# Longformer attention and an MoE layer on one core: where bias adds, gathers, stores and roundings stand in the order

## The chip, the cores and the metric

The kernel runs on one core of one Trainium2 chip. A core has TensorE (PE, matmuls), VectorE (DVE), ScalarE (ACT), GpSimd (POOL) and SyncE (SP, which here only issues transfers); each works through a queue of its own in program order, and semaphores make one wait for another. Matmuls write PSUM, the other engines move results from there to SBUF. The metric is the device time of one execution in microseconds (us). Before the change three timed runs took 341.11 us in the median (341.09 to 342.33).

## The reference

Attention over q, k, v of shape (8, 8, 576, 64) with a mask: a query sees keys within 32 positions, and 8 global positions see and are seen by all. The result, as 4608 tokens of 512, goes through two dense layers with a squared ReLU between them.

```python
mask = np.abs(pos[:, None] - pos[None, :]) <= window          # window = 32
mask = mask | is_global[:, None] | is_global[None, :]
scores = np.where(mask, scale * (q @ k.T), -1e9)
attn = softmax(scores);  x = attn @ v                          # per head
h = x @ w_in                                                   # 512 -> 2048
g = s * np.maximum(h, 0.0) ** 2 + b
out = g @ w_out                                                # 2048 -> 512
```

## The kernel before

The work on attention runs over 32 pairs of heads (four pairs to one of the 8 batches), each pair in 8 steps that are called s = 0 to 7 here. The dense layers are cut into 9 blocks of 512 tokens; a block is 16 pieces that make a slice of h (`psh`, L728), which ACT passes through ReLU into `r` (L750) and DVE squares into `g` (L753), and 16 pieces that multiply by w_out (`pso`, L762). These pieces are called quanta; `Q` puts one or more of them between the steps of attention, so that PE has work while the other engines do exp, masks and evictions. All engines are scheduled by hand: what stands earlier in the program stands earlier in the engine's queue.

A pair's way: its q and k rows are loaded by SP (`load_nat`, `load_q`, L213 and L234), rounded to bf16 by ACT (`round_k` L224 into `natb`, `round_q` L249 and L254 into `sixq`), and transposed, the keys of pairs from 8 on by a transposing transfer of SP (`turn_k`, L260, into `kt`), the queries by PE (`trans_b`, L538 into `pst`) with an eviction by DVE (L581, L576). `put_kq` (L513) puts the global columns in with two tiny DVE copies. PE makes the scores in two parts (`qk`, L605 into `pss`), ACT takes the exp (L616, L614 into `em`), DVE applies the mask (L617), and `put_out` (L633) makes weighted sums and row sums of two pairs into `po`, of which there is one tile. ACT makes the reciprocal by Ln and Exp (L687, L690), DVE sums the global queries' parts (L657 and on) and scales the result into `xt` (L680), the transposed tokens of three batches. The global queries' rows are made apart and put into `xt` by eight small POOL copies per batch (`scatter`, L705); the dense layers read `xt`. Up to pair 5 the transposes of the queries share the PSUM tile of the scores.

The constant b adds a row to the output: b times the column sums of w_out. The sums are made on the side. POOL loads eight pieces of w_out (`wst`, L1064, in two buffers), 15 adds collect them in `wsum` (L1066, L1068, one to a step of pairs 12 to 16), and at pair 18 a matmul with ones makes `bias_row` of it (L1074). Until then finished output tiles are held in SBUF (`osbh`, `sixk`); from pair 19 on `release` adds the row to one of the 12 held tiles (L1079, DVE) and stores it (L1080, POOL).

Rows of q and k at the global positions of the next two batches are fetched by POOL (`gather`, L356, into `gf`). POOL also stores the finished tiles (L786), casts some v tiles (L273) and puts global v rows into the ring of v tiles (`put_v`, L505).

In the loop over pairs, `at(s, f)` has f issued after step s of the pair, and the lists above it say which pair does what at which step.

Of the kernel before, what the change touches and what calls it, by code (L numbers as in the profile page):

```python
# [34 lines left out]
NPAIR = B * H // 2  # L35
# [8 lines left out]
NDUO = 11  # L44
# [28 lines left out]
def view(ap, *dims):  # L73

    return bass.AP(
        tensor=ap.tensor, offset=ap.offset, ap=[list(ap.ap[0])] + [list(d) for d in dims]
    )
# [3 lines left out]
def kernel(  # L81
# [12 lines left out]
    nc = tc.nc  # L94
# [63 lines left out]
    for t, eng in (("k", nc.sync), ("q", nc.scalar)):  # L158
        eng.dma_start(
            out=six0[t].rearrange("p (h x) -> p h x", h=2),  # L160
# [8 lines left out]
    wsum = wpool.tile([P, DM], FP32)  # L169
# [15 lines left out]
    def v_slot(p):  # L185
        return p - 2 if p in (4, 5) else (p if p < 4 else p - 2) % NV
# [71 lines left out]
    def turn_k(p):  # L258
        kts[p] = kqp.tile([P, KT0 + NCH * P], BF16, tag="kt", name="kt")
        nc.sync.dma_start_transpose(  # L260
            out=kts[p][:, KT0:].rearrange("p (c x) -> p c x", x=P), in_=natb[:, p % NV]
        )
# [6 lines left out]
    def load_v(eng, p):  # L269
        load_nat(eng, "v", p)  # L270

    def cast_v(eng, p):
        eng(out=vring[:, p % NVR], in_=(natk if p in (4, 5) else natv)[:, v_slot(p)])  # L273
# [13 lines left out]
    for t in "kq":  # L287
# [5 lines left out]
        out=natv[0:NG].rearrange("p n c h d -> p (n c h d)"),  # L293
# [6 lines left out]
        out=natk[0:NG, 2:4].rearrange("p n c h d -> p (n c h d)"),  # L300
# [6 lines left out]
        out=natk[KC:P, 0:2].rearrange("p n c h d -> p (n c h d)"),  # L307
# [13 lines left out]
    for p in range(6):  # L321
# [4 lines left out]
        out=gidx_1[:].rearrange("p (a b) -> p a b", b=NG), in_=view(row[:], [0, P // NG], [1, NG])  # L326
# [6 lines left out]
        out=part[:], in0=rowi[:], scalar1=3, scalar2=7,  # L333
# [5 lines left out]
        out=half[:], in0=partf[:], scalar=2.0 * S, in1=half[:], op0=OP.mult, op1=OP.add  # L339
# [115 lines left out]
    def flush():  # L455
        ops, later[:] = list(later), []
        for f in ops:
            f()
# [252 lines left out]
    held_rows = []  # L711
# [88 lines left out]
    def Q(n=1):  # L800
        for _ in range(n):
            if quanta[0] > 0:
                quanta[0] -= 1
                next(moe)
# [112 lines left out]
    def turned(f, p):  # L917
        ops = []
        f(p, ops)
        return ops[0]  # L920
# [13 lines left out]
        out=sel6[:], in0=view(idx6[:], [1, NJ], [0, NG]),  # L934
        in1=view(gidx_f, [0, NJ], [1, NG]), op=OP.is_equal,
# [110 lines left out]
    lead()  # L1046
    qk(4, 1)
    quanta[0] = 32
    Q(2)
    flush()  # L1050
    q_out = turned(trans_b, 5)
    k_out = turned(trans_a, 5)
    q_out()
    k_out()
    cast_v(A, 4)
    for i in (1, 2, 3):
        rows_of(i)
# [4 lines left out]
    def wpiece(j):  # L1062
        wt = stage.tile([P, 2, DM], FP32, tag="wst", name="wst")
        nc.gpsimd.dma_start(out=wt[:], in_=w_out2[:, 2 * j : 2 * j + 2])  # L1064
        if j == 0:
            return [lambda: nc.vector.tensor_add(out=wsum[:], in0=wt[:, 0], in1=wt[:, 1])]  # L1066
        return [
            lambda i=i: nc.vector.tensor_add(out=wsum[:], in0=wsum[:], in1=wt[:, i])  # L1068
            for i in range(2)
        ]  # L1070

# [11 lines left out]
    for p in range(4, NPAIR):  # L1083
        bi, hp = divmod(p, 4)
        ex = {}

        def at(s, f, *a, ex=ex):
            ex.setdefault(s, []).append(lambda: f(*a))

        nq = [1] * 8  # L1090
        if bi == 1:
            nq = [0, 1, 1, 1, 1, 1, 1, 1] if hp else [0, 0, 0, 0, 0, 0, 0, 1]
            if hp > 1:
                nq[(1, 4)[hp - 2]] = 0
        elif hp == 0:
            quanta[0] += 32
        if p > 7 and hp != 3 and p + 2 <= NDUO + 1:
            turn_k(p + 2)
        if p + 3 > NDUO + 1 and p + 3 < NPAIR:
            at(5, turn_k, p + 3)  # L1100
            if p + 3 >= NTQ:
                at(5, turn_q, p + 3)
        for j in {4: (8,), 5: (9,), 6: (10,), 7: (11, 12)}.get(p, (p + 5,)):
            if j < NPAIR:
                if j in (10, 11, 12):
                    x = {10: 1, 11: 4, 12: 5}[j]
                    at(x, load_nat, nc.sync, "k", j)
                    at(x, load_q, j)
                elif j > 8:
                    load_nat(nc.sync, "k", j)  # L1110
                    load_q(j)
                if p < 6:
                    load_v(nc.sync, j)
                else:
                    at(5, load_v, nc.sync, j)
        if p == 5:
            for i in range(NG):
                nc.gpsimd.dma_start(
                    out=gvall[i : i + 1].rearrange("o (b h d) -> o b h d", b=B - 2, h=H),
                    in_=v[2:, :, ds(greg_p[i], 1), :].rearrange("b h o d -> o b h d"),  # L1120
                )
        if p % 8 == 4 and 4 < p and p + 4 < NPAIR:
            at(2 if p > NDUO else 6, gather, (p + 4) // 8)
        if p >= 6 and p + 2 < NPAIR:

            todo = {8: (11,), 9: (12,)}.get(
                p, {0: (p + 3, p + 4), 2: (p + 3,), 3: (p + 2, p + 3)}.get(hp, ())
            )
            if hp == 2 and p + 3 < NDUO:
                todo = ()  # L1130
            if hp == 3 and p + 2 > NDUO:
                todo = (p + 3,)
            for i, j in enumerate(todo):
                if j < NPAIR:
                    x = 4 if p in (8, 9) else 4 * i
                    at(1 + x, round_k, j)
                    at(3 + x, round_q, j)
            if hp == 3 and p + 2 < NDUO:
                at(3, turn_k, p + 2)
        if p == 6:  # L1140
            at(3, round_k, 8)
            at(4, turn_k, 8)
            at(7, round_q, 8)
        if p == 7:
            at(7, put_v, None, 8)
        if p >= 7 and p + 2 < NPAIR:
            at(7, put_v, None, p + 2)
        if p % 8 > 4 and p + 3 < NPAIR:
            if p % 8 == 6:
                steps = globals_of((p + 4) // 8)  # L1150
                at(7 if p < NDUO else 2, steps[0])
                if p > NDUO:
                    at(4, steps[1])
            elif p % 8 == 7 and p < NDUO:
                at(3, steps[1])
        for s in {12: (2, 3, 4), 13: (7,), 14: (2, 4, 7)}.get(p, (2, 3, 4, 7)):
            if adds:
                at(s, adds.pop(0))
        if p in (11, 12, 14, 15):
            for j in range(2):  # L1160
                at(6, lambda i: adds.extend(wpiece(i)), 2 * (11, 12, 14, 15).index(p) + j)
        if p == 18:
            assert not adds
            at(2, bias)
        if p > 18 and hp in (0, 3) and held_rows:
            at(2, release)
            at(6, release)
        run_pair(p, nq, ex)
# [42 lines left out]
```

## Time and profile before

| | |
|---|---|
| timed runs | 341.09, 341.11, 342.33 us |
| the profiled execution, in all | 343.69 us |
| its span, first to last instruction | 342.1 us |
| mean granted clock of TensorE | 0.995 |
| PE busy | 326.8 us (96%) |
| ACT, DVE, POOL busy | 208.4, 206.1, 85.4 us |
| moved by transfers | 52.54 MB, 154 GB/s in the mean |

The time outside the span, 1.6 us in the profiled execution, is start and end of the program. PE's busy share is high in every stretch after the first 50 us; the transfer engines are busy up to about 250 us and hardly after it. A busy PE is not a PE at its peak, since the ends of matmuls are modelled, so the places where it stands still are looked up one by one, with the engine that each was waiting for.

### The profile page before, as it was taken

Reading aid. Unit: us, or ns where it says so; the run is one execution under the profiler, and the core shown is the slowest. Engines: PE = TensorE matmul, PEld = TensorE weight load, DVE = VectorE, ACT = ScalarE, POOL = GpSimd, SP = SyncE. Lnnn points to the kernel's source line nnn. Section 1 sums busy time; section 2 is a strip of 40 time slices with the busy share of each in tenths; the row PEclk is TensorE's granted clock in tenths of the full one; section 3 lists DMA queues with packets and bytes.
Section 4 is the critical chain, followed back from the end, with each engine's and each line's share of the span. In section 5 each row is a group of like instructions: output and inputs, shape, how many; then the busy total and the mean of one; then the engine's idle time right before and its main releaser. Section 6 shows DMA issues by size and latency. Waiting matters only on the chain.

```text
span 342.1 us, 8736 instructions
## 1 busy us (share of the span) xinstructions
PE 326.8 (96%) x3364; PEld 169.3 (49%) x3364; DVE 206.1 (60%) x537; ACT 208.4 (61%) x372; POOL 85.4 (25%) x190
## 2 busy tenths in 40 slices
PE   7998799799999999999999999999999999999996
PEld 4555344344444544457744444444467544444444
DVE  5488677454766787867675767576757434423422
ACT  3556778544996498549874997499548415503600
POOL 7563733116000401050028102700350030000000
PEclk9999999899999999999999999999999999999999
DMA  9999999899998899999799979996540011011002
GB/s 153 193 192 204 199 197 200 192 200 208 180 178 182 215 172 236 208 185 174 149 237 234 229 150 227 253 182 146 150 138 2 0 67 58 3 61 63 2 35 87
DMA packets 132309, 52.54 MB, mean 154 GB/s; under 512 B 120915, under 2 KB 127363, under 8 KB 132259
## 3 DMA queue, kind: packets, MB, share of 16 engines
q1 hardware_dynamic: 121129, 33.27, 54.0%
q0 software_dynamic: 10784, 18.29, 22.6%
q8 instruction: 26, 0.43, 0.6%
q10 hardware_dynamic: 354, 0.43, 0.4%
q14 instruction: 16, 0.13, 0.2%
HBM read 42.35 MB, written 9.44 MB: 151 GB/s over the span
## 4 chain that ended last, share of the span: by engine, by line
PE 69%; issue 8%; ACT 6%; DVE 5%; DMA 5%; POOL 4%; SPq 2%; POOLq 0%; ACTq 0%; DVEq 0%
PE pso L762 30%; PE psh L728 27%; PE po L633 4%; PE pss L605 3%; DMA natq<-in_q_dram 3%; SPq L213 2%; POOL xt L705 2%; ACT r L750 2%; DMA wst<-in_moe_w_out_dram 2%; PE pst L544 1%; ACT em L616 1%; DVE g L753 1%; ACT em L614 1%; PE psg L894 1%; PE pst L538 1%
## 5 line engine op out<-in xcount | busy, mean ns | idle before, releaser
L728 PE MATMUL psh<-xt,win_t 128*128 128x512 bf16 (+2 forms) x704 | 132.3, 341 | 3.2 <-POOL xt L705 2.7
L762 PE MATMUL pso<-wout_t,g 128*128 128x512 bf16 (+1 forms) x592 | 131.0, 377 | 0.0
L750 ACT ACTIVATE r<-psh 128x512 bf16<-128x512 f32 x144 | 85.3, 605 | 71.3 <-PE psh L728 68.1
L728 PEld LDWEIGHTS <-win_t 128*128 128x128 bf16 x704 | 63.0, 98 | 60.7 <-issue 4.8
L762 PEld LDWEIGHTS <-g 128*128 128x128 bf16 x592 | 56.7, 99 | 64.3 <-issue 1.9
L753 DVE TENSOR_TENSOR g<-r 128x512 bf16<-128x512 bf16 x144 | 62.5, 439 | 41.9 <-ACT r L750 40.8
L617 DVE TENSOR_TENSOR em<-em,mask 128x904 bf16<-128x904 bf16 x64 | 38.7, 611 | 30.6 <-ACT em L616 23.9
L616 ACT ACTIVATE em<-pss 128x840 bf16<-128x840 f32 (+1 forms) x41 | 36.3, 885 | 31.1 <-PE pss L605 31.1
L782 DVE SCALAR_TENSOR_TENSOR osb<-pso,sb,bias_row 128x512 f32<-128x512 f32 (+1 forms) x25 | 18.2, 728 | 33.4 <-PE pso L762 33.1
L705 POOL COPY xt<-xg 128x4 bf16 (+1 forms) x72 | 16.9, 235 | 55.9 <-DVE xt L680 52.1
L680 DVE TENSOR_TENSOR xt<-po,rep 128x480 bf16<-128x480 f32 (+2 forms) x60 | 24.4, 449 | 0.5 <-ACT rep L690 0.5
L605 PE MATMUL pss<-qt,kt 64*128 64x160 bf16 (+1 forms) x366 | 19.6, 234 | 3.3 <-DVE grow L343 1.4
L605 PEld LDWEIGHTS <-kt 64*128 64x128 bf16 x384 | 12.2, 99 | 20.9 <-issue 14.3
L786 POOL DMA_DIRECT2D out_dram<-osb x16 | 8.9, 557 | 44.0 <-DVE osb L782 43.1
L614 ACT ACTIVATE em<-pss 128x452 bf16<-128x452 f32 x40 | 19.7, 553 | 0.0
L224 ACT CAST natb<-natk 128x640 bf16<-128x640 f32 x24 | 17.7, 737 | 0.5 <-DMA natk<-in_k_dram 0.5
L633 PE MATMUL po<-em,vring 128*32 128x160 bf16 (+3 forms) x840 | 17.5, 221 | 0.0
L687 ACT ACTIVATE ln<-po 128x324 f32<-128x324 f32 (+1 forms) x30 | 13.2, 439 | 4.8 <-PE po L633 4.8
L690 ACT ACTIVATE rep<-ln 128x324 f32<-128x324 f32 (+1 forms) x32 | 15.0, 470 | 0.3
L249 ACT CAST sixq<-natq 128x640 bf16<-128x640 f32 (+1 forms) x19 | 14.2, 746 | 0.0
L633 PEld LDWEIGHTS <-vring 128*32 128x32 bf16 x896 | 13.9, 100 | 0.1
L273 ACT CAST vring<-natv 128x640 bf16<-128x640 f32 x19 | 13.8, 732 | 0.0
(124 smaller groups left out, 233.8 us busy)
## 6 DMA issues: line engine op xcount, KB each, us to landing
natv<-in_v_dram SPq DMA_DIRECT2D x59, 150.0 KB
natk<-in_k_dram SPq DMA_DIRECT2D x47, 150.0 KB
wst<-in_moe_w_out_dram POOLq DMA_DIRECT2D x8, 512.0 KB, 5.1
out_dram<-osb POOLq DMA_DIRECT2D x16, 256.0 KB, 3.0
natq<-in_q_dram SPq DMA_DIRECT2D x54, 75.0 KB
out_dram<-osbh POOLq DMA_DIRECT2D x9, 256.0 KB, 3.7
win_t<-in_moe_w_in_dram POOLq DMA_DIRECT2D x4, 512.0 KB
wout_t<-in_moe_w_out_dram POOLq DMA_DIRECT2D x4, 512.0 KB, 11.3
```

Of the source, the lines that this page charges most:

```text
L605: nc.tensor.matmul(ps[hh][:, at : at + hi - lo], ktile[p][r, P * c : P * c + P], qbufs[p % 3][r, lo:hi], start=at == 0, stop=at + hi - lo ...
L614: nc.scalar.activation(em[:, hh], ps[hh][:, 0:n], AF.Exp, scale=SCALE)
L616: nc.scalar.activation(em[:], both[:, :, 0:n], AF.Exp, scale=SCALE)
L617: later.append(lambda: nc.vector.tensor_mul(em[:], em[:], masks[g]))
L633: nc.tensor.matmul(po[DH * j : DH * j + DH, a : a + n], view(vring[:, p % NVR, c, hh, part - 1 :], [2, DH]) if part else onesb[:], emt[(p, ...
L680: nc.vector.tensor_tensor(out=view(xt[:, 2 * g, x0 + t0 :], [NXT, 2], [w, runs], [1, w]), in0=view(po[:, STEP[blk] + col :], [STEP[blk], 2 ...
L705: nc.gpsimd.tensor_copy(out=xt[:, h, S * (bi % NX) : S * (bi % NX) + S][:, :, ds(greg_p[i], 1)], in_=xgs[bi][:, h, i : i + 1],)
L728: nc.tensor.matmul(psh[:, d0 : d0 + n], win_t[:, a, f * P : f * P + P], xt[:, a, x0 : x0 + n], start=(a == 0 and j == 0), stop=(a == 3), s ...
L750: nc.scalar.activation(r[:], psh, AF.Relu)
L753: later.append(lambda g=g, r=r: nc.vector.tensor_mul(g[:], r[:], r[:]))
L762: nc.tensor.matmul(pso[:, 0:nn], gl[f][:, u * P : u * P + P], wout_t[:, f, n0 : n0 + nn], start=(f == 0), stop=(f == 15),)
L782: nc.vector.scalar_tensor_tensor(out=osb[:, 0:nn], in0=pso[:, 0:nn], scalar=s_bc, in1=bias_row[:, n0 : n0 + nn], op0=OP.mult, op1=OP.add,)
```

## The change

Four edits to the order, no change to what is computed.

- Pair 5's transposes move between the two quanta that stood ahead of them, and the flush of pair 4's masks and squares comes after.
- The 15 adds of w_out's rows go from DVE to POOL; at pairs 14 and 15 their steps become (2, 4, 5) and (2, 3, 4, 5).
- `gather` moves from pairs 12 and 20 to pairs 11 and 19; of the releases, those of the first pair of a batch (20, 24, 28) move to its second pair (21, 25, 29).
- Pairs 9 and 10: before, pair 7 rounded k and q of pair 9 at steps 1 and 3 and of pair 10 at steps 5 and 7. Now the steps are 1 and 5 for pair 9, 7 for k of pair 10, and step 2 of pair 8 for its q.

```diff
     quanta[0] = 32
-    Q(2)
-    flush()
+    Q(1)
     q_out = turned(trans_b, 5)
     k_out = turned(trans_a, 5)
     q_out()
     k_out()
+    Q(1)
+    flush()
     cast_v(A, 4)
...
-            return [lambda: nc.vector.tensor_add(out=wsum[:], in0=wt[:, 0], in1=wt[:, 1])]
+            return [lambda: nc.gpsimd.tensor_add(out=wsum[:], in0=wt[:, 0], in1=wt[:, 1])]
         return [
-            lambda i=i: nc.vector.tensor_add(out=wsum[:], in0=wsum[:], in1=wt[:, i])
+            lambda i=i: nc.gpsimd.tensor_add(out=wsum[:], in0=wsum[:], in1=wt[:, i])
             for i in range(2)
         ]
...
-        if p % 8 == 4 and 4 < p and p + 4 < NPAIR:
-            at(2 if p > NDUO else 6, gather, (p + 4) // 8)
+        if p % 8 == 3 and 4 < p and p + 5 < NPAIR:
+            at(4, gather, (p + 5) // 8)
...
+            if p == 7:
+                at(1, round_k, 9)
+                at(5, round_q, 9)
+                at(7, round_k, 10)
+                todo = ()
+            if p == 8:
+                at(2, round_q, 10)
...
-        for s in {12: (2, 3, 4), 13: (7,), 14: (2, 4, 7)}.get(p, (2, 3, 4, 7)):
+        for s in {12: (2, 3, 4), 13: (7,), 14: (2, 4, 5), 15: (2, 3, 4, 5)}.get(p, (2, 3, 4, 7)):
...
-        if p > 18 and hp in (0, 3) and held_rows:
+        if p > 18 and hp in (1, 3) and held_rows:
```

The order of ACT's instructions at pairs 7 and 8. `em_1389` and `em_1426` are the exps of pair 7's two halves, the casts into `natb` are keys and those into `sixq` queries. First before:

```order
L616 ACTIVATE em_1389<-pss 128x904
L273 CAST vring<-natv 128x640
L224 CAST natb<-natk 128x640
L254 CAST sixq<-natq 96x2x6x64
L616 ACTIVATE em_1426<-pss 128x840
L687 ACTIVATE ln<-po 128x324
L224 CAST natb<-natk 128x640
L690 ACTIVATE rep<-ln 128x324
L254 CAST sixq<-natq 96x2x6x64
L616 ACTIVATE em_1536<-pss 128x904
```

And now (`em_1425` and `em_1535` are the same two exps, numbered anew):

```order
L616 ACTIVATE em_1389<-pss 128x904
L273 CAST vring<-natv 128x640
L224 CAST natb<-natk 128x640
L616 ACTIVATE em_1425<-pss 128x840
L687 ACTIVATE ln<-po 128x324
L254 CAST sixq<-natq 96x2x6x64
L690 ACTIVATE rep<-ln 128x324
L224 CAST natb<-natk 128x640
L616 ACTIVATE em_1535<-pss 128x904
L687 ACTIVATE ln<-po 128x292
L254 CAST sixq<-natq 96x2x6x64
```

The queries of pair 9 are now cast behind the exp and the Ln; the keys of pair 10 one place later; the queries of pair 10 behind the first exp of pair 8.

The order of POOL's instructions from the copies of the scatter of batch 2 (the last of them is the first row) to the first copy of that of batch 3. Before:

```order
L705 COPY xt<-xg 128x4
L1064 DMA wst<-in_moe_w_out_dram 128x2x512 x2
L273 CAST vring<-natv 128x640
L1064 DMA wst<-in_moe_w_out_dram 128x2x512 x4
L705 ISA
L705 COPY xt<-xg 128x4
```

And now:

```order
L705 COPY xt<-xg 128x4
L1065 DMA wst<-in_moe_w_out_dram 128x2x512 x2
L273 CAST vring<-natv 128x640
L1069 TENSOR_TENSOR wsum<-wsum,wst 128x512 x4
L1065 DMA wst<-in_moe_w_out_dram 128x2x512 x2
L1069 TENSOR_TENSOR wsum<-wsum,wst 128x512 x4
L1065 DMA wst<-in_moe_w_out_dram 128x2x512 x2
L1069 TENSOR_TENSOR wsum<-wsum,wst 128x512 x3
L705 ISA
L705 COPY xt<-xg 128x4
```

Eleven of the 15 adds now stand between the two scatters, three stand ahead of the first and one behind the second.

The order of DVE's instructions at the turn of pair 5 (`em_951`, `em_978`: masks of pair 4; `g_984` and the next: squares of the first quanta; `pst`: the transposed keys). Before:

```order
L617 TENSOR_TENSOR em_951<-em_951,mask_452 128x904
L617 TENSOR_TENSOR em_978<-em_978,mask_456 128x840
L753 TENSOR_TENSOR g_984<-r 128x512
L753 TENSOR_TENSOR g_989<-r 128x512
L556 COPY kt<-pst 128x5x120
L513 COPY kt<-gkt 128x5x8
L513 COPY qt_119<-gqt_120 128x5x8
```

And now:

```order
L556 COPY kt<-pst 128x5x120
L513 COPY kt<-gkt 128x5x8
L513 COPY qt_119<-gqt_120 128x5x8
L617 TENSOR_TENSOR em_951<-em_951,mask_452 128x904
L617 TENSOR_TENSOR em_978<-em_978,mask_456 128x840
L753 TENSOR_TENSOR g_984<-r 128x512
L753 TENSOR_TENSOR g_1019<-r 128x512
```

The eviction of the keys and the two small copies, which PE awaits, stand ahead of the four multiplications.

## Rows read from the trace of the kernel before

**Rows 1.** The page, engines and a costly group: busy us (share), and mean ns.
```profile
PE 326.8 (96%) x3364; PEld 169.3 (49%) x3364; DVE 206.1 (60%) x537; ACT 208.4 (61%) x372; POOL 85.4 (25%) x190
...
L753 DVE TENSOR_TENSOR g<-r 128x512 bf16<-128x512 bf16 x144 | 62.5, 439 | 41.9 <-ACT r L750 40.8
```
**Rows 2.** Waits of PE over the span: waiter, releaser, us, times, longest.
```profile
PE psh L728 <- POOL xt L705: 2.7, 4, 1.3
PE pst L538 <- ACT em L616: 2.1, 2, 1.8
```
**Rows 3.** Timeline, 60 to 70 us: start, length, instruction, idle time before it.
```profile
60.47 0.36 PE L605 MATMUL pss<-qt,kt 64*128 64x92 bf16 x6
...
61.73 0.83 ACT L254 CAST sixq<-natq 96x768 bf16<-96x768 f32 x1 [1.19 <-DMA natq<-in_q_dram]
...
62.47 0.86 ACT L616 ACTIVATE em<-pss 128x840 bf16<-128x840 f32 x1
...
63.38 0.61 PE L538 MATMUL pst<-ident,sixq 96*128 96x96 bf16 x6 [1.83 <-ACT em L616]
...
63.78 5.14 PE L762 MATMUL pso<-wout_t,g 128*128 128x512 bf16 x16
...
65.62 0.18 DVE L513 COPY kt<-gkt 128x40 bf16<-128x40 bf16 x1 [0.82 <-DMA kt<-natb]
...
67.09 0.84 DVE L680 TENSOR_TENSOR xt<-po,rep 128x120 bf16<-128x120 f32 x2
...
69.16 0.37 PE L633 MATMUL po<-em,onesb 128*32 128x92 bf16 x12
...
69.83 1.90 PE L762 MATMUL pso<-wout_t,g 128*128 128x512 bf16 x8
```
**Rows 4.** One stretch: length, busy us of each engine, granted clock, DMA, GB/s.
```profile
64.00:68.00 4.00, 4.00 (x13) 1.54 (x12) 3.09 (x8) 1.82 (x3) 0.46 (x1) 0.64 0.95 179
```
**Rows 5.** Timeline at the turn of pair 5.
```profile
39.77 1.54 POOL L445 DMA_DIRECT2D wout_t<-in_moe_w_out_dram  x2
...
40.85 0.46 DVE L513 COPY kt<-gkt 128x40 bf16<-128x40 bf16 x1
...
41.39 0.37 PE L605 MATMUL pss<-qt,kt 64*128 64x160 bf16 x6 [1.43 <-DVE grow L343]
```
**Rows 6.** The tile of w_out's pieces: ns min/median/max, and transfers to landing.
```profile
L1068 DVE TENSOR_TENSOR wsum<-wsum,wst x14: 677/684/693, 109.8 to 149.1; 128x512 f32<-128x512 f32 x14
...
DMA to landing us min/median/max: 5.1/5.1/5.1
```
**Rows 7.** Timeline from the scatter of batch 2 to that of batch 3.
```profile
112.21 2.44 POOL L705 COPY xt<-xg 128x4 bf16 x8 [28.94 <-DVE xt L680]
...
137.27 0.69 DVE L1068 TENSOR_TENSOR wsum<-wsum,wst 128x512 f32<-128x512 f32 x1 [2.18 <-DMA wst<-in_moe_w_out_dram]
...
140.99 0.56 PE L605 MATMUL pss<-qt,kt 64*128 64x92 bf16 x12 [0.70 <-DVE qt L576]
...
147.50 2.89 POOL L705 COPY xt<-xg 128x4 bf16 x8 [4.80 <-DVE xt L680]
...
150.44 0.95 PE L728 MATMUL psh<-xt,win_t 128*128 128x320 bf16 x7 [0.26 <-POOL xt L705]
```
**Rows 8.** Timeline, a cast of POOL and a square of DVE at one time.
```profile
58.35 0.72 POOL L273 CAST vring<-natv 128x640 bf16<-128x640 f32 x1 [1.57 <-DMA natv<-in_v_dram]
...
58.53 0.82 DVE L753 TENSOR_TENSOR g<-r 128x512 bf16<-128x512 bf16 x1 [0.85 <-ACT r L750]
```
**Rows 9.** Timeline around the scatter of batch 4.
```profile
179.85 1.01 POOL L356 DMA_INDIRECT gf<-in_k_dram,grow  x1 [0.30 <-issue]
...
180.14 0.79 DVE L680 TENSOR_TENSOR xt<-po,rep 128x480 bf16<-128x480 f32 x2
...
182.73 2.08 POOL L705 COPY xt<-xg 128x4 bf16 x8
...
184.86 1.46 PE L728 MATMUL psh<-xt,win_t 128*128 128x512 bf16 x6 [0.55 <-POOL xt L705]
```

## Prediction

> **What bounds the kernel now.** I read the page first, then the waits of PE, then the span in stretches, then the timeline of the few places where PE stands still. PE is busy for 96% of the span, the next engine for 61% [rows 1]. So the time is PE's stream plus its holes, and a change that touches no matmul can only close holes or open new ones. The list of PE's waits shows how little there is: 2.7 us on the scatter copies of POOL, 2.1 us on an exp of ACT [rows 2]. Two of the four waits for copies, 0.26 and 0.55 us, come back below.
>
> The largest hole after the start is at 61.55 us. PE has sent the scores of pair 7's second half [rows 3] and next turns the queries of pair 8 into the same PSUM tile, which the exp of those scores must first empty. The exp stands in ACT's queue behind the rounding of pair 9's queries, and that waits 1.19 us for its load. So the exp runs at 62.47 instead of about 60.9, and PE idles 1.83 us. When it resumes, its granted clock is low (0.64 on average from 64 to 68 us [rows 4]): sixteen matmuls take 5.14 us, where at full clock eight take 1.90, so sixteen about 3.6 [rows 3].
>
> **Rounding later, pairs nine and ten.** The move puts the exp ahead of the queries' rounding (order of ACT above). The exp then starts at 60.9, takes 0.86, and PE resumes at about 61.8, 1.6 us earlier; at full clock its sixteen matmuls would end near 65.7 instead of 68.85. That looks like 3.1 us. What is late next takes most of it away. The scores of pair 8 need its transposed keys, whose transfer DVE awaits until 65.62 [rows 3]; the transfers ahead of it on SP are neither moved nor fewer, so I leave it there. Behind that wait DVE's queue holds the mask, an eviction, the sums and two scalings of the output tile, the last ending at 67.93 (67.09 plus 0.84). PE's next weighted sum writes that same output tile (there is one), so it cannot start before 67.95. In the profiled execution it started at 69.16. The gain against that execution is 69.16 − 67.95 = 1.2 us, not 3.1. In an execution of the old kernel whose clock stays high, the same sixteen matmuls end near 67.4 (63.78 + 3.6), the scores come at once, and the weighted sum waits for the same 67.95: there the move gains nothing. The key rounding of pair 10 moves behind one small ACT operation and had to wait for its load anyway; the queries of pair 10 are rounded some 3 us later, in a stretch where ACT is idle. Both at 0.
>
> The timed runs were 341.09, 341.11 and 342.33. The third stands 1.22 above the median, close to the 1.2 us that the low clock costs above, so I take the two low ones for runs without it. No row proves that; if wrong, the median gains 1.2 more. The working below is made on the profiled execution (343.69 in all, 342.1 of it span) and its differences are set against the median of 341.11.
>
> **Pair five between two quanta.** DVE evicts pair 5's keys ahead of two masks and two squares instead of behind them (order of DVE above), and PE's 1.43 us hole before 41.39 [rows 5] can shrink. What ended it is two tiny copies on DVE, 0.46 us where the same copy takes 0.18 at 65.62; they finish just as POOL's run of transfer issues does (39.77 + 1.54 = 41.31). That run does not move. So the gain is between 0 and 0.9 us, I take 0.3; but all of it ends in front of the transposed keys at 65.62, so it is worth 0 at the end.
>
> **The sums of w_out's rows, fifteen adds from DVE to POOL.** On DVE each takes 0.68 us [rows 6], 10.3 us in all, and one of them makes DVE wait 2.18 us for its data at 137.27 [rows 7]. Behind it stand the masks and the eviction of queries that PE awaits for 0.70 us at 140.99. With the add gone, DVE has no reason to be late there: gain 0.70. Two more adds (1.37 us) stand before the sums that feed the scatter of batch 3, which starts at 147.50 and ends 0.26 us too late for PE at 150.44. DVE would be ready about 2 us earlier. Gain 0.26, if POOL is ready too.
>
> That is the price to settle, since POOL now does the adds in front of that scatter (order of POOL above). No row shows a two-input operation on POOL. From below: its cast of 640 elements takes 0.72 [rows 8], so 512 elements with one input take 0.58. From above: two such passes and a cast's length of 640 each, 1.44, plus a wait of 0.44 for a square of DVE in the way [rows 1], 1.88. I take two passes of 0.58 and some 0.2 of waiting, 1.35, since it is twice the nearest row's work. POOL's chain after the scatter of batch 2: DVE has two adds less ahead of that one too, so it starts near 110.8 rather than 112.21 [rows 7] and ends near 113.1; the first load is issued some 0.4 later; each pair of loads is a wait of about 5.5 (5.1 from issue to landing [rows 6], the rest hand-over); then 4, 4 and 3 adds. 113.5 + 3 × 5.5 + 11 × 1.35 = 144.9. The scatter needs 2.1 to 2.9 and PE would need it by 149.5 (150.44 less 0.26 and 0.70), so there are some 2 us to spare. The first three adds come early, near 86 to 90 us, far ahead of their scatter. The adds also get in DVE's way: a square that coincides with a POOL cast took 0.82 instead of 0.44 [rows 1, 8]. For the three adds near 88 us, where ACT and DVE set PE's pace, that is at most 3 × 0.4 = 1.2 us, at least 0; I take 0.2, since DVE has short waits of its own there. Elsewhere DVE has lost 10.3 us of work, and this covers it.
>
> The Trainium skill, page GPSIMD Engine Reference, section 4.1 Engine selection, speaks against such a move: it calls a two-input elementwise operation about twice as slow there as on VectorE, and its section 3.1 gives 4497 ns for 2048 elements. By that an add would be about 1.12 us, an estimate; the chain would end at 142.3 and the result would not change. The page SBUF — State Buffer, section Who interferes with whom, says that a VectorE instruction with two SBUF inputs and a GpSimd instruction that reads SBUF shut each other out for a whole instruction; the square of 0.82 us agrees with that.
>
> **Gathers and stores away from the scatters.** For the scatter of batch 4, POOL issues two gathers from 179.85 on and a store before the copies start at 182.73, although DVE had the data at 180.93 (180.14 plus 0.79); PE loses 0.55 us at 184.86 [rows 9]. In the new order the gathers stand one pair earlier, and the store one pair later. The scatter can then begin near 181 and PE does not wait: gain 0.55. Scatters 5 and 6 cost PE nothing now. The twelve held rows' adds and stores lose no work; those that move to the second pair of a batch fall among the squares, where two adds of 0.68 us in 16 us of DVE can delay a square by less than the reserve of three buffers. I take 0, between 0 and 0.3 for each of three batches.
>
> **Sum.** 0.70 + 0.26 + 0.55 − 0.2 = 1.3 us. 341.11 − 1.3 = 339.8. Against the profiled execution it is 1.3 + 1.2 = 2.5.
>
> **Rivals.**
> 1. The low clock counts. If the 341.1 runs hold it too and it is gone afterwards, the time is 339.8 − 1.2 = 338.6. For it: the one trace there is shows it. Against it: the two timed runs that lie 1.2 lower than the third.
> 2. The hole only moves, and the clock falls at its new place. PE will now idle about 0.2 at 65.7 and 1.7 before 67.95, as much as the 1.83 after which the clock fell; but after 1.43 us before 41.39 it stayed at its higher level. The fall costs some 1.5 us (5.14 − 3.6 for sixteen matmuls): 339.8 + 1.5 = 341.3.
> 3. POOL becomes late, and the kernel slower. The point is where 113.5 + 16.5 + 11 T + 2.2 passes 149.5, at T = 1.57 us for an add. At the upper bound, 1.88, PE waits 3.4 us: 339.8 + 3.4 = 343.2. For it: adds, loads and scatter stand in one queue, and each add waits for the one before. Against it: POOL is idle three quarters of the time, and 1.57 is 2.7 times the one-input price.
> 4. DVE was never the cause of 0.70 and 0.26, and they reappear elsewhere: then 0.55 is left, 340.6.
>
> **How the numbers follow.** My case 0.42, rival 1 0.19, rival 2 0.22, rival 3 0.08, rival 4 0.09. About 0.5%, 1.7 us, is what a measurement can tell from no change: 339.4 and 342.8 are the borders. Faster: nearly all of rival 1 and under half of my own case (it lies 0.4 above the border), with 0.02 of the rest: 0.37. Slower: rival 3 in part, and mishaps of rival 2 with a dear add: 0.10. Same: 0.53. The range runs from 338.2, rival 1 with a little more, to 341.9, rival 2 with its own spread; outside stay most of rival 3 and some of rival 1's tail. My case alone runs from 339.1 to 340.6.
>
> **What would show it.** Right: no idle of PE at 140 and 184, an add on POOL between 1.1 and 1.5 us, the scatter of batch 3 waiting for DVE and not for an add, and near 67 us PE waiting for DVE's scaling rather than for the exp. Wrong: the transposed keys of pair 8 landing well before 65 us, which would free the 3 us; adds above 1.57 us; or a low granted clock after 68 us.

## The result and the profile after

The change makes the kernel slower. Twenty executions of the changed kernel have a median of 346.20 us (341.88 to 349.31), twenty of the kernel before 341.31 us (339.73 to 344.11). The ratio of comparable runs is 1.009, with an interval of 1.0061 to 1.012; the eight highest runs of the changed kernel, the profiled one among them, are left out of it, as disturbed, which is why it is below the ratio of the medians (346.20/341.31 = 1.014). The prediction was 339.8 in a range from 338.2 to 341.9, so both the sign and the range were wrong.

The profiled execution of the changed kernel took 347.55 us, 345.9 of them span, at a mean granted clock of 0.989 (before: 343.69, 342.1, 0.995). The page first: the engines, DVE's squares and masks and the new adds, busy us and mean ns.

```profile
PE 322.0 (93%) x3322; PEld 169.3 (49%) x3364; DVE 203.9 (59%) x522; ACT 208.7 (60%) x372; POOL 104.3 (30%) x205
...
L753 DVE TENSOR_TENSOR g<-r 128x512 bf16<-128x512 bf16 x144 | 66.1, 467 | 41.2 <-ACT r L750 40.2
...
L617 DVE TENSOR_TENSOR em<-em,mask 128x904 bf16<-128x904 bf16 x64 | 41.0, 648 | 28.8 <-ACT em L616 23.2
...
L1069 POOL TENSOR_TENSOR wsum<-wsum,wst 128x512 f32<-128x512 f32 x14 | 19.1, 1364 | 12.0 <-DMA wst<-in_moe_w_out_dram 11.2
```

Against [rows 1], POOL has 18.9 us more. DVE lost 15 adds worth 10.3 us and yet is only 2.2 us less busy (206.1 to 203.9): most of the other 8 us came back as longer instructions. The 144 squares alone went from 62.5 to 66.1 us, the 64 masks from 38.7 to 41.0. That is the first sign, and it stands on the page.

The waits of PE over the span (waiter, releaser, us, times, longest):

```profile
PE pss L605 <- DVE qt L513: 3.2, 9, 0.8
PE pss L605 <- DVE qt L576: 2.4, 1, 2.4
...
PE po L633 <- DVE xt L680: 1.7, 1, 1.7
PE psh L728 <- POOL xt L705: 1.3, 1, 1.3
```

The waits on the scatter copies went from 2.7 us in four places to 1.3 in one [rows 2], as the gathers' move and the DVE terms wanted for two of them; a third, 0.61 us at 37.76, which no term named, is gone wherever pair 5's transposes were moved, and is there with the adds alone (0.61) and the roundings alone (0.61). In their stead stand a single hole of 2.4 us on DVE's eviction L576, and one of 1.7 on the scaling L680. The first line is nine short waits, of which 0.76 us at 39.33 and 0.54 at 95.56 come up below.

Where the 2.4 us come from, in the timeline from 119 to 131 us (start, length, instruction, idle time before it). DVE:

```profile
119.63 1.33 DVE L617 TENSOR_TENSOR em<-em,mask 128x904 bf16<-128x904 bf16 x1 [0.28 <-ACT em L614]
120.88 2.89 DVE L753 TENSOR_TENSOR g<-r 128x512 bf16<-128x512 bf16 x2
123.70 0.22 DVE L657 TENSOR_REDUCE gs<-po 128x24 f32<-128x72 f32 x1
123.84 0.83 DVE L680 TENSOR_TENSOR xt<-po,rep 128x120 bf16<-128x120 f32 x2
```

POOL beside it, and PE behind it:

```profile
118.77 6.12 POOL L1069 TENSOR_TENSOR wsum<-wsum,wst 128x512 f32<-128x512 f32 x4 [3.01 <-DMA wst<-in_moe_w_out_dram]
...
121.32 1.89 PE L728 MATMUL psh<-xt,win_t 128*128 128x512 bf16 x8
125.61 0.55 PE L605 MATMUL pss<-qt,kt 64*128 64x92 bf16 x12 [2.40 <-DVE qt L576]
...
127.67 3.50 PE L728 MATMUL psh<-xt,win_t 128*128 128x512 bf16 x10 [0.22 <-issue]
```

The same stretch of DVE before the change:

```profile
119.12 0.63 DVE L617 TENSOR_TENSOR em<-em,mask 128x904 bf16<-128x904 bf16 x1 [0.28 <-ACT em L614]
119.66 0.42 DVE L753 TENSOR_TENSOR g<-r 128x512 bf16<-128x512 bf16 x1
120.51 0.43 DVE L753 TENSOR_TENSOR g<-r 128x512 bf16<-128x512 bf16 x1 [0.43 <-ACT r L750]
```

POOL had waited 3.01 us for w_out's pieces, and then ran four adds back to back for 6.12 us. Beside them a mask takes 1.33 us instead of 0.63 and two squares 2.89 instead of 0.85. DVE gets about one instruction with two inputs from SBUF through for each add. The second add and the first of the two squares, each by itself:

```profile
120.55 1.53 POOL L1069 TENSOR_TENSOR wsum<-wsum,wst 128x512 f32<-128x512 f32 x1
120.88 1.49 DVE L753 TENSOR_TENSOR g<-r 128x512 bf16<-128x512 bf16 x1
```

The square ends at 122.37, some 0.3 us behind the end of the add (122.08): it waited for all that was left of the add. The add in its turn, behind the mask, took 1.53 us, where the shortest of its kind takes 1.26. The two engines take turns, one instruction each. A tiny copy of DVE from SBUF, with one input, is held up as well; it takes 0.17 us elsewhere, and ended with the last add before scatter 3 (144.97):

```profile
144.35 0.65 DVE L513 COPY kt<-gkt 128x40 bf16<-128x40 bf16 x1
```

The sums and the scaling, which read PSUM, keep their times (0.22 and 0.83). All that runs beside the four adds stands in DVE's queue ahead of the eviction that PE's next scores need, so PE finishes its eight matmuls near 123.2 and waits 2.40 us. After the hole the clock falls (length, busy us of PE, PEld, DVE, ACT and POOL, granted clock, DMA, GB/s):

```profile
127.00:130.50 3.50, 3.28 (x9) 1.25 (x9) 1.70 (x4) 2.43 (x6) 0.00 (x0) 0.57 0.97 294
130.50:134.00 3.50, 3.50 (x21) 1.52 (x19) 3.03 (x8) 3.04 (x6) 3.33 (x3) 1.00 1.35 158
```

So in the first stretch PE ran mostly at the lower level of 1.2 GHz: ten matmuls take 3.50 us where eight take 1.89 at full clock, about 1.1 us lost. In the second, at full clock again, POOL runs the next four adds; the squares beside them are long again, but PE does not wait for DVE there.

The place of the rounding, near 66 us, in the same timeline:

```profile
62.29 0.42 PE L538 MATMUL pst<-ident,sixq 96*128 96x96 bf16 x6 [1.02 <-ACT em L616]
62.55 3.62 PE L762 MATMUL pso<-wout_t,g 128*128 128x512 bf16 x15
66.16 0.17 DVE L513 COPY kt<-gkt 128x40 bf16<-128x40 bf16 x1 [2.63 <-DMA kt<-natb]
66.47 0.37 PE L605 MATMUL pss<-qt,kt 64*128 64x160 bf16 x6 [0.30 <-DVE qt L513]
67.62 0.84 DVE L680 TENSOR_TENSOR xt<-po,rep 128x120 bf16<-128x120 f32 x2
68.52 0.51 PE L633 MATMUL po<-em,onesb 128*32 128x92 bf16 x12 [1.68 <-DVE xt L680]
70.06 2.65 PE L762 MATMUL pso<-wout_t,g 128*128 128x512 bf16 x7 [0.33 <-issue]
```

Set beside [rows 3], the hole of 1.83 us on the exp is down to 1.02, the matmuls behind it run at full clock (fifteen in 3.62 us, where sixteen took 5.14), and a new hole of 1.68 stands before the weighted sum, because DVE still waits until 66.16 for the transposed keys. The low clock moved with the hole: the mean from 68 to 72 us is 0.57.

```profile
68.00:72.00 4.00, 3.15 (x45) 1.77 (x47) 1.69 (x3) 1.13 (x2) 0.72 (x1) 0.57 1.22 200
```

### The profile page after: what moved, and what is told of

Same layout as the page of the kernel before. It is cut to its first block, busy times and chain, and to the rows that moved or that the text cites. A ratio compares the mean times of both kernels' runs of the same rounds, so it can differ in the third digit from the quotient of the medians.

```text
span 345.9 us, 8689 instructions
## 1 busy us (share of the span) xinstructions
PE 322.0 (93%) x3322; PEld 169.3 (49%) x3364; DVE 203.9 (59%) x522; ACT 208.7 (60%) x372; POOL 104.3 (30%) x205
## 4 chain that ended last, share of the span: by engine, by line
PE 53%; DMA 14%; issue 13%; POOL 8%; ACT 3%; DVE 3%; SPq 3%; POOLq 0%; ACTq 0%; DVEq 0%
PE pso L762 26%; PE psh L728 20%; DMA wst<-in_moe_w_out_dram 6%; PE po L633 3%; DMA natv<-in_v_dram 3%; POOL wsum L1069 3%; SPq L213 2%; PE pss L605 2%; DMA natk<-in_k_dram 2%; DMA sixk<-in_k_dram 2%; POOL gf L356 1%; POOL xt L705 1%; ACT em L614 1%; DMA gvall<-in_v_dram 1%; DVE xt L680 1%
## 5 line engine op out<-in xcount | busy, mean ns | idle before, releaser
L728 PE MATMUL psh<-xt,win_t 128*128 128x512 bf16 (+4 forms) x687 | 131.6, 342 | 2.9 <-POOL xt L705 1.3
L762 PE MATMUL pso<-wout_t,g 128*128 128x512 bf16 (+1 forms) x572 | 127.1, 375 | 2.6 <-issue 2.2
L753 DVE TENSOR_TENSOR g<-r 128x512 bf16<-128x512 bf16 x144 | 66.1, 467 | 41.2 <-ACT r L750 40.2
L617 DVE TENSOR_TENSOR em<-em,mask 128x904 bf16<-128x904 bf16 x64 | 41.0, 648 | 28.8 <-ACT em L616 23.2
L705 POOL COPY xt<-xg 128x4 bf16 (+1 forms) x72 | 14.4, 200 | 42.0 <-DVE xt L680 38.2
L605 PE MATMUL pss<-qt,kt 64*128 64x160 bf16 (+1 forms) x366 | 20.3, 235 | 7.1 <-DVE qt L513 3.2
L680 DVE TENSOR_TENSOR xt<-po,rep 128x480 bf16<-128x480 f32 (+2 forms) x60 | 24.5, 449 | 0.5 <-ACT rep L690 0.5
L1069 POOL TENSOR_TENSOR wsum<-wsum,wst 128x512 f32<-128x512 f32 x14 | 19.1, 1364 | 12.0 <-DMA wst<-in_moe_w_out_dram 11.2
L1081 POOL DMA_DIRECT2D out_dram<-osbh x9 | 5.0, 554 | 42.3 <-DVE osbh L1080 37.6
```

What stands on the lines that cost most here:

```text
L605: nc.tensor.matmul(ps[hh][:, at : at + hi - lo], ktile[p][r, P * c : P * c + P], qbufs[p % 3][r, lo:hi], start=at == 0, stop=at + hi - lo ...
L617: later.append(lambda: nc.vector.tensor_mul(em[:], em[:], masks[g]))
L680: nc.vector.tensor_tensor(out=view(xt[:, 2 * g, x0 + t0 :], [NXT, 2], [w, runs], [1, w]), in0=view(po[:, STEP[blk] + col :], [STEP[blk], 2 ...
L728: nc.tensor.matmul(psh[:, d0 : d0 + n], win_t[:, a, f * P : f * P + P], xt[:, a, x0 : x0 + n], start=(a == 0 and j == 0), stop=(a == 3), s ...
L753: later.append(lambda g=g, r=r: nc.vector.tensor_mul(g[:], r[:], r[:]))
L762: nc.tensor.matmul(pso[:, 0:nn], gl[f][:, u * P : u * P + P], wout_t[:, f, n0 : n0 + nn], start=(f == 0), stop=(f == 15),)
```

## Experiments

Theory A: the adds cost the time, since they hold up DVE's instructions that read two rows of SBUF, for about the length of an add each; PE waits behind them. Rival B: the rounding costs it, through the hole that moved and the low clock behind it. A third possibility is the prediction's rival 3: POOL itself is late for the scatters.

**The adds alone.** The kernel before with only this edit:

```diff
-            return [lambda: nc.vector.tensor_add(out=wsum[:], in0=wt[:, 0], in1=wt[:, 1])]
+            return [lambda: nc.gpsimd.tensor_add(out=wsum[:], in0=wt[:, 0], in1=wt[:, 1])]
...
-        for s in {12: (2, 3, 4), 13: (7,), 14: (2, 4, 7)}.get(p, (2, 3, 4, 7)):
+        for s in {12: (2, 3, 4), 13: (7,), 14: (2, 4, 5), 15: (2, 3, 4, 5)}.get(p, (2, 3, 4, 7)):
```

> The old kernel with the 15 adds on POOL at their new steps, nothing else. Theory A (the adds hold up DVE's two-input multiplications, squares and masks, for their whole length of 1.36 us, and PE ends up waiting for DVE's evictions near 120 to 130 us): 3 to 5 us slower than before, 344.5 to 346.5, squares near 119 to 124 us taking over 1 us, a wait of PE of 2 us or more on DVE's eviction of queries there. Theory B (the loss comes from the hole near 67 us and the low clock behind it): within 1 us of before, 340.5 to 342.

Measured: 344.21 us, just under the range of theory A, ratio 1.0093 (1.0061 to 1.0124), as much as the whole change. Its timeline repeats that of the changed kernel:

```profile
115.73 5.71 POOL L1068 TENSOR_TENSOR wsum<-wsum,wst 128x512 f32<-128x512 f32 x4 [3.35 <-DMA wst<-in_moe_w_out_dram]
117.44 2.89 DVE L753 TENSOR_TENSOR g<-r 128x512 bf16<-128x512 bf16 x2
122.17 0.55 PE L605 MATMUL pss<-qt,kt 64*128 64x92 bf16 x12 [2.39 <-DVE qt L576]
```

Behind this hole the clock stayed at 1.00 (124 to 128 us), so the low clock does not follow it each time.

**All but the adds.** The changed kernel with the adds on DVE at their old steps (the same lines the other way round).

> The new kernel with the adds back on DVE at their old steps; pair five, roundings, gathers and stores stay as in the change. Theory A: the loss is gone, 339.5 to 341.5, no wait of PE over 1 us after 75 us. Theory B: slower than before by 2 us or more, 343 to 346, with the wait near 67 us and a low clock behind it in most runs.

Measured: 341.89 us, ratio 1.0006 (0.9978 to 1.0035). No PE wait of 2.4 us on L576; the waits on L680 (1.68 us at 67.94) and, at 147.33, 0.28 on the scatter are there. The loss is gone, as theory A wants, but the time is 0.4 us above the top of its range (339.5 to 341.5): the gain that this range held beside it is not seen. Both runs point to theory A.

**Each add in four pieces of 128 columns.**

```diff
+    def quarters(one, two):
+        for x in range(0, DM, DM // 4):
+            c = slice(x, x + DM // 4)
+            nc.gpsimd.tensor_add(out=wsum[:, c], in0=one[:, c], in1=two[:, c])
```

> The new kernel with each add on POOL made in four of 128 columns (60 instructions, the same data). Theory A in its form 'one instruction holds DVE off until it ends': DVE gets its turn every 0.4 us or so, squares near 120 us take at most 0.9 us, and some 2 us of the loss come back: 342.5 to 344.5. Rival (the two engines share a fixed rate, or the adds' amount of data is what counts): as slow as the new kernel, 345 to 347, with squares as long in sum. POOL's adds together become longer, about 0.45 us each quarter.

Measured: 343.43 us, ratio 1.0066 (1.0036 to 1.0097). What waits longest is another thing now. Timeline of DVE, PE and POOL, then a PE wait:

```profile
117.04 1.27 DVE L753 TENSOR_TENSOR g<-r 128x512 bf16<-128x512 bf16 x2
120.17 0.83 PE L605 MATMUL pss<-qt,kt 64*128 64x92 bf16 x12 [0.20 <-DVE qt L576]
...
142.29 4.98 POOL L1066 TENSOR_TENSOR wsum<-wsum,wst 128x128 f32<-128x128 f32 x12 [3.73 <-DMA wst<-in_moe_w_out_dram]
147.22 2.03 POOL L705 COPY xt<-xg 128x4 bf16 x8
...
PE psh L728 <- POOL xt L705: 3.7, 2, 2.4
```

Shorter pieces hold a square up for less (0.63 each instead of 1.45), and PE's 2.40 us are down to 0.20. But a piece takes 0.45 us, an add 1.8, and now the last twelve pieces stand right in front of scatter 3, with no idle time between, and PE waits 2.4 us for that. This is the prediction's rival 3, whose threshold was 1.57 us for an add, made to happen. In the changed kernel itself it did not happen: the scatter at 149.66 had POOL idle for 4.70 us, waiting for DVE.

**The roundings alone.** The kernel before with

```diff
+            if p == 7:
+                at(1, round_k, 9)
+                at(5, round_q, 9)
+                at(7, round_k, 10)
+                todo = ()
+            if p == 8:
+                at(2, round_q, 10)
```

> The old kernel with only pairs nine and ten rounded later. My account of the hole: PE resumes at about 62 us instead of 63.4, then waits about 1.7 us for DVE's scaling until 68 us, since the transposed keys of pair 8 land at 65.6 as before; the time stays within 0.7 us of before, 340.5 to 342. Rival (the exp was the bound there): 338 to 339. Rival (the moved hole brings the low clock more often or at a worse place): 342 to 343.5.

Measured: 342.73 us, ratio 1.0033 (1.0008 to 1.0059): a small loss, outside my range and inside that of the last rival, the low clock at the moved hole. In the profile the hole moves as in the changed kernel and the matmuls behind the new place are slow:

```profile
67.56 0.49 PE L633 MATMUL po<-em,onesb 128*32 128x92 bf16 x12 [1.68 <-DVE xt L680]
69.07 2.67 PE L762 MATMUL pso<-wout_t,g 128*128 128x512 bf16 x7 [0.33 <-issue]
```

"All but the adds" holds the same roundings and stands at 1.0006, so rival B is at most a small part of the loss.

**What in an add does it.** In two kernels each add is replaced, and the sums of w_out's rows are left out: by a memset, which reads nothing, and by a copy, which reads one row. The steps are those of the change. First the memsets:

```diff
-            return [lambda: nc.gpsimd.tensor_add(out=wsum[:], in0=wt[:, 0], in1=wt[:, 1])]
-        return [
-            lambda i=i: nc.gpsimd.tensor_add(out=wsum[:], in0=wsum[:], in1=wt[:, i])
-            for i in range(2)
-        ]
+            return [lambda: nc.gpsimd.memset(wsum[:], 0.0)]
+        return [lambda i=i: nc.gpsimd.memset(wt[:, i], 0.0) for i in range(2)]
```

And the copies:

```diff
-            return [lambda: nc.gpsimd.tensor_add(out=wsum[:], in0=wt[:, 0], in1=wt[:, 1])]
+            return [lambda: nc.gpsimd.tensor_copy(out=wsum[:], in_=wt[:, 0])]
...
-            lambda i=i: nc.gpsimd.tensor_add(out=wsum[:], in0=wsum[:], in1=wt[:, i])
+            lambda i=i: nc.gpsimd.tensor_copy(out=wsum[:], in_=wt[:, i])
```

> The changed kernel with a GpSimd memset of 128x512 in the place of each of the 15 adds (the sums of w_out's rows are left out). Each memset writes SBUF and reads nothing. Theory A1 (the adds hold up DVE's squares and masks because both read two rows of SBUF): the squares near 118 and 131 us stay at 0.40 to 0.45 us, PE does not wait 2.4 us on L576, and the time is that of the changed order with the adds on DVE, 341.9 within 0.8. Rival A2 (any work of GpSimd in SBUF beside them does it, read or write): squares of 0.6 us and more beside the memsets, and a time above 343.

> The changed kernel with a one-input GpSimd copy (128x512, f32 to f32) in the place of each add (the sums are left out). Each copy reads one row of SBUF and writes one, and should take about 0.6 us after the cast of 640 elements in 0.72. Theory A1 (a GpSimd instruction that reads SBUF holds up a DVE instruction with two inputs from SBUF for its whole length): squares beside the copies take up to 0.42 + 0.6 = 1.0 us, but four copies are over in 2.4 instead of 5.5 us, so some four squares late by 0.4 each and a time between 342 and 343.5. Rival A3 (it takes GpSimd's two inputs as well): squares stay at 0.45 us, time 341.9 within 0.8.

Measured: memsets 341.73 us, ratio 0.9996 (0.9968 to 1.0025); copies 341.71 us, 0.9974 (0.9939 to 1.001). The profiled execution of the copies took 345.88 us, the longest of its ten; only what single instructions did beside each other is read from it. First the squares beside memsets, from 112 to 140 us (ns min/median/max), then a memset and a cast of DVE from SBUF to SBUF, then copies with the square and the masks near them, merged (x2) and single (x1):

```profile
L753 DVE TENSOR_TENSOR g<-r x16: 411/425/426, 113.6 to 130.5; 128x512 bf16<-128x512 bf16 x16
```

```profile
123.42 0.52 POOL L1068 MEMSET wst<- 128x512 f32 x1
123.49 0.53 DVE L470 CAST gb<-gf 128x128 bf16<-128x128 f32 x1
```

```profile
117.33 1.47 POOL L1069 COPY wsum<-wst 128x512 f32<-128x512 f32 x2 [4.72 <-DMA wst<-in_moe_w_out_dram]
118.00 0.79 POOL L1069 COPY wsum<-wst 128x512 f32<-128x512 f32 x1
117.90 0.42 DVE L753 TENSOR_TENSOR g<-r 128x512 bf16<-128x512 bf16 x1 [0.43 <-ACT r L750]
...
122.05 1.58 POOL L1069 COPY wsum<-wst 128x512 f32<-128x512 f32 x2 [3.25 <-DMA wst<-in_moe_w_out_dram]
122.77 0.86 POOL L1069 COPY wsum<-wst 128x512 f32<-128x512 f32 x1
122.16 1.00 DVE L617 TENSOR_TENSOR em<-em,mask 128x840 bf16<-128x840 bf16 x1
123.08 1.03 DVE L617 TENSOR_TENSOR em<-em,mask 128x904 bf16<-128x904 bf16 x1
```

No square is late beside a memset: writing alone does not hold a square up. It is not harmless to all of DVE, though: the cast at 123.49 takes 0.53 us, to just behind the end of the memset, where it takes 0.22 elsewhere.

Copies hold DVE up as adds do, each for the rest of its own length: the two masks take 1.00 and 1.03 us instead of 0.60 and 0.63. The square at 117.90 seems to run through amid two copies, but it began as the first of them ended, and the second was the one that waited: 0.79 us, where the shortest copy takes 0.61. So theory A1's hold-up is there, and only its price in time, 342 to 343.5, was too high. By the traces an add is worse because it is longer: a square beside pieces of 0.45 us takes 0.63, beside copies up to 0.72, beside adds of 1.26 and more up to 1.52. No run varied the number of inputs at one length.

The Trainium skill, page SBUF — State Buffer, section Who interferes with whom, says that a VectorE instruction with two SBUF inputs contends with a GpSimd instruction that reads SBUF, and not with one that only writes it. The squares and masks beside adds (1.45 and 1.33 us), memsets (0.42 and 0.63) and copies agree.

**Pair five and the gathers alone.** The kernel before with the diff's parts for these two.

```diff
-    Q(2)
-    flush()
+    Q(1)
...
-        if p % 8 == 4 and 4 < p and p + 4 < NPAIR:
-            at(2 if p > NDUO else 6, gather, (p + 4) // 8)
+        if p % 8 == 3 and 4 < p and p + 5 < NPAIR:
+            at(4, gather, (p + 5) // 8)
```

> The kernel before with two of the four edits alone: pair five's transposes between the two quanta, and the gathers one pair earlier with the releases in the second pair of a batch. My prediction gave 0.55 us for the gathers (PE's idle time at 184.86 us gone) and 0 for pair five (scores of pair five up to 0.9 earlier, all of it lost in front of the transposed keys of pair eight at 65.6). By that the ratio to the kernel before is 0.998, with no wait of PE on a scatter copy between 180 and 190 us. Rival: the releases fall among the squares and give 0.3 us back in each of three batches, ratio 1.001. Rival: pair five's earlier start is kept, ratio 0.996.

Measured: 341.84 us, ratio 0.9991 (0.9963 to 1.0019). PE's 0.55 us at 184.86 [rows 9] are gone in this trace. The same holds for all seven traces with the gathers moved, and in the two others it is there (0.54 us with the adds alone, 0.53 with the roundings alone). The time can't tell 0.998 from 1.001.

**A transfer issued earlier.** "All but the adds", and SP issues the transposing transfer of pair 8's keys ahead of pair 10's loads instead of behind them:

```diff
-                    x = {10: 1, 11: 4, 12: 5}[j]
+                    x = {10: 5, 11: 4, 12: 5}[j]
```

> The three other edits with the adds on DVE as before, and one edit of mine: the loads of pair ten's keys and queries are issued on SP behind the transposing transfer of pair eight's keys, not ahead of it. Without it that transfer was issued at 61.68 us although its data was ready at 54.4, and DVE waited for it 2.47 us, to 65.58; behind it stood the scaling for which PE waited 1.68 us at 67.94. Theory (the transposed keys bound this place, and the rounding gains nothing until they come earlier): the transfer is issued near 59, DVE's copy comes near 63, PE's wait of 1.68 at the weighted sum is gone, and the time falls by 1.5 to 2.4 us against the same kernel without the edit, to 339.5 to 340.4 and a ratio of 0.993 to 0.996 to the kernel before. Rival: the transfer lands no earlier (the transfer engines are busy for over 90% there), and the time stays at 341.9 within 0.7. Rival: the loads of pair ten, 2 us later, make ACT's rounding and the exp behind it late, and the time is above 342.5.

Measured: 340.52 us, ratio 0.9967 (0.9939 to 0.9996): below the kernel before and the changed one. SP, DVE and PE in its timeline:

```profile
56.74 2.63 SPq L260 DMA_TRANSPOSE kt<-natb  x1
61.69 0.18 DVE L513 COPY kt<-gkt 128x40 bf16<-128x40 bf16 x1
64.28 0.37 PE L605 MATMUL pss<-qt,kt 64*128 64x160 bf16 x6
64.58 0.37 PE L633 MATMUL po<-em,onesb 128*32 128x92 bf16 x12
```

The transfer is issued five microseconds earlier (56.74 against 61.68), DVE no longer waits for it, and PE goes from the scores straight into the weighted sum: the hole of 1.68 us is gone, and the mean clock of this profile is 1.000. The gain against "all but the adds" is 1.4 us by the medians (341.89 to 340.52), a little under the 1.5 expected. The two were measured in different sessions, and their intervals overlap by a little. Of its twelve executions 8 keep a mean clock of 0.998 or more, against 1 of twelve in "all but the adds". That agrees with the hole bringing the low clock, but the kernel before too had more such executions in the second session (14 of 35) than in the first (8 of 29).

## Why the prediction was wrong

**The step that failed** is the sentence on the adds getting in DVE's way: "at most 3 × 0.4 = 1.2, at least 0; I take 0.2", with "Elsewhere DVE has lost 10.3 us of work, and this covers it". The adds alone make the kernel 0.93% slower, some 3.2 us (0.0093 of 341.78; 2.1 to 4.2 by the interval). The prediction had −0.76 for the same edit (0.2 − 0.70 − 0.26), so it is off by about 4 us there. For the whole change it had −1.3, and the ratio of 1.009 makes it about +3.1: of these 4.4 us the adds are nearly all. Three errors are in the step.

- The size of one collision. The 0.4 came from [rows 8], a square beside a cast of 0.72 us. But the add had just been priced at 1.35, and what holds DVE up lasts as long as the POOL instruction. By the prediction's own number a square could be held up by as much as 1.35; the trace shows 1.0 (1.45 for 0.42). The rule that the prediction takes from the Trainium skill (SBUF — State Buffer, Who interferes with whom), that the two shut each other out for a whole instruction, already said so, and was not carried through into the sum. The section has the words "for the whole instruction" of VectorE's two-port modes, and calls the lock exclusive for every contention; that it is the whole instruction for two SBUF inputs too is what the traces here show.
- The number of them. Counting only the three adds near 88 us left out twelve. Near 95 to 97 us, behind the first three, PE lost 0.54 and 0.49 us in the changed kernel where it lost 0.30 at 96.87 before: 0.7 us, inside the bounds given. The hole of 2.40 us came from the next four, and in this profile the low clock behind it cost another 1.1.
- The cover. The 10.3 us that DVE was rid of lie spread over five pairs, one add to a step. The adds on POOL wait for their data and then run in a row, whatever steps they were given: four in 6.12 us. In those 6 us DVE had one add less to do, 0.68 us [rows 6], and three instructions that were 0.7 to 1.0 us longer each. A credit summed over 40 us was set against a debt due within 6.

**The price of an add** was right: 1.35 taken, 1.364 measured (1.257 to 1.706, the long ones behind an instruction of DVE). The Trainium skill's figure (GPSIMD Engine Reference, section 3.1) made 1.12 of it, an estimate; the shortest here is 1.257. The chain to scatter 3 held as well: the adds end at 144.97 (140.75 plus 4.22) where 144.9 was forecast, and the scatter waits for DVE. Part of that is luck, since the three waits for loads came to 15.6 us instead of 16.5 and the eleven adds to 15.8 instead of 14.9. Rival 3 did not happen, but the quarters, at 1.8 us, crossed its threshold.

**The three small gains** are there in the trace of the change: PE no longer stands still at 140.99, 150.44 and 184.86. That the gathers' move brought the third is shown by every trace, as said above. That the adds' move brought the other two is not shown so clearly. In the four kernels with the adds on DVE, PE waits on L576 there for 0.53, 0.40 and 0.71 us in three (the roundings alone, pair five with the gathers, the earlier transfer) and not at all in "all but the adds"; for scatter 3 it waits in two (0.28 and 0.32) and not in the others. With the adds alone on POOL 0.31 on L576 is left. So rival 4 is not borne out, and not excluded either. The timed runs do not show the 1.5 us: with memsets, where all three holes are gone, the ratio is 0.9996 (0.9968 to 1.0025); the loss of the roundings may hide them.

**The rounding**: the mechanism was right to a tenth. The weighted sum waits for the scaling (predicted 1.7 before it, measured 1.68), the scores come at once or nearly (0.30), but the price, taken as 0, measured alone is a loss of 0.3 to 2.0 us (0.0008 to 0.0059 of 341.78). What the forecast left to rival 2, the clock falling at the new place, did happen, in the profiles of the changed kernel and of the roundings alone. It did not in that of "all but the adds", with the same hole of 1.68; so the hole makes the fall possible, not certain.

**The assumption on the clock of the timed runs** is not borne out. Of the 29 executions of the kernel before that were timed beside the first four experiments, 8 have a mean granted clock of 0.998 or more and a median of 341.12; 18 have about 0.995 and 342.05. So the median run does hold a low stretch, and it goes with some 0.9 more. Of the twelve executions of the changed kernel that enter the ratio, the 6 at the high clock have a median of 344.38, the 6 others 345.20. So some 3.3 us are lost with no help from the clock, and 0.8 more with it.

**Pair five**: the scores start at 39.33 with 0.76 us of idle time before them, where it was 1.43 [rows 5]; worth nothing at the end that these runs can tell (0.9991 together with the gathers), as taken.

**What was not followed up** in the prediction: it named the transposed keys as what bounds the weighted sum, and took their transfer as fixed. SP's queue before the change shows that its data was ready at 54.0 and that it was issued at 61.98, behind the loads of pair 10. With it moved, and the adds left on DVE, the other three edits come out ahead of the kernel before, by 0.04 to 0.6%.

The rows for this, from the kernel before:

```profile
53.27 0.75 ACT L224 CAST natb<-natk 128x640 bf16<-128x640 f32 x1
...
58.20 2.80 SPq L213 DMA_DIRECT2D natk<-in_k_dram  x2
61.05 0.83 SPq L234 DMA_DIRECT2D natq<-in_q_dram  x1
61.98 1.33 SPq L260 DMA_TRANSPOSE kt<-natb  x1
```

## What to carry to other kernels

Moving elementwise work to GpSimd is not free because GpSimd is idle: instructions of DVE that read SBUF may each have to wait for the end of the GpSimd instruction beside them, so price the move at one GpSimd instruction's length for each such collision, in the few microseconds where the work will really run, and not by DVE's mean load. Work that waits for a load runs in a burst when the load lands, whatever steps it was given; look for what PE needs from DVE behind that burst. Where a hole would only move to the next wait, follow that wait to its issue: an in-order queue of transfers may hold it for no reason of data.

## What the runs showed of the hardware

- Adds of 128x512 f32 on GpSimd (1.36 us) stretched DVE's bf16 squares from 0.42 to 1.45 us and more, a mask from 0.63 to 1.33 and a copy of 40 columns from 0.17 to 0.65: what DVE began inside such an add ended just behind the add's end, and an add that began inside an instruction of DVE grew from 1.26 to as much as 1.71. Copies (0.61 us at the least) did the same over their own length.
- Memsets of the same size (0.52 us) stretched no square and no mask, but one cast from SBUF to SBUF, from 0.22 to 0.53. DVE's instructions that read PSUM kept their times beside all of them.
- A quarter of such an add takes 0.442 us at the least, over a third of the 1.257 of a whole: by (4 × 0.442 − 1.257) / 3 some 0.17 us of each instruction do not depend on its size, an estimate.
- The same hole of 1.68 us before the same weighted sum was followed by the lower clock in two profiles (0.57 and 0.62 of full speed over 4 us) and not in a third (1.00).
